# First four x tiles by row loads and TensorE turning instead of transposing loads, with new orders for all engines

## The chip, the cores and the metric

The kernel runs on one core of one Trainium2 chip. The metric is device time in microseconds (us), the median of several runs. A core has TensorE (PE, with PEld for its weight loads), VectorE (DVE), ScalarE (ACT), GpSimd (POOL) and SyncE (SP), which here only issues DMAs; ACT issues some too. Every engine works through its own list in order and waits on semaphores.

## The reference, cut to what matters

x has 2048 rows of D = 448. Part A is attention with a memory over 4 segments of 512 rows and 16 heads of 28; part B is a token-mixing MLP over normalised x; a gate mixes both.

```python
q, k, v = heads(x @ wq), heads(x @ wk), heads(x @ wv)      # 16 heads, 4 segments
p = softmax(qs @ ks.T * scale + causal_mask)               # per segment and head
a_dot = p @ vs
a_mem = (phi(qs) @ M) / (phi(qs) @ z + 1e-6)               # phi(t) = t+1 if t>0 else exp(t)
o = sigmoid(beta) * a_mem + (1 - sigmoid(beta)) * a_dot
M, z = M + phi(ks).T @ vs, z + sum(phi(ks))                # after each segment
a = o @ wo
h = layernorm(x)                                           # over D, no weights
b = (gelu(h.T @ w1 + b1) @ w2 + b2).T                      # w1: 2048 x 1792, w2: 1792 x 2048
g = sigmoid(sum(x * gate_w))
out = g * a + (1 - g) * b                                  # bf16, 1 x 2048 x 448
```

## The kernel before, in words

The kernel is one straight program. Each piece of work is an `op` with a name, the resources it reads and writes, and a body; `ORDER` lists, engine by engine, the names in the order in which they are issued. Where a name is followed by `@` and digits these are the PSUM banks or buffers it takes; `*n` repeats a name with its last number counted up. A planner outside this file, with costs and due times of its own, wrote these lists; the file only follows them and adds the semaphore waits that the resources ask for.

x is needed in two forms. Rows (`xh`, 16 tiles of 128 rows; `ldx4` loads tiles 4 to 7) feed the layer norm: `bns`, `bna` (statistics), `vpe`, `rstd`, `nmr` (coefficients) and `ln{t}`, which normalises tile t in place for the MLP. Turned (`xT`, columns of x on partitions, in four pieces c of 128 columns starting at 0, 128, 256 and 320, and four groups tc of 512 rows) it feeds the projections. Before the change `transpose_x(tc)` (L548) fills group tc by two transposing DMAs on SP, `dtx{tc}_0` (c = 0 to 2) and `dtx{tc}_1` (c = 3).

Weights: `ldwv0`, `ldwv1`, `ldwv2`, `ldwvb` (L538, L542) load wv in four parts by c on ACT's queue, `ldwk*` and `ldwq*` wk and wq, mostly on SP's; `padk`, `padx`, `padq` on DVE (L675) spread wk and wq into the padded form `wqk`. `ldgw` loads the gate's weights, `gtr` turns them on PE, `gw` copies them beside wv. `ldb1`, `ldb2` (L568, L570) load the biases on ACT's queue into a stage that `szb` on POOL clears first; `szg` clears the gate's stage; `btr` turns the biases. `v0`, `v1` set constants in the v buffer, `id0`, `id1` make the identity matrix `ident`.

PE names: `warm`, `warm2` are dummy matmuls (L664); `pra{t}`, `prb{t}`, `prt{t}` are the passes over c = 0, c = 1 and the last whole c of the value projection of row tile t; `lot{t}` is the half-row pair that does the remaining 64 rows of the contraction for tiles t and t+1 at once. `prk`, `prq`, `prx`, `lok`, `loq`, `pra0_g` are the same for keys, queries and the spread last dims. `sc` are scores (28-row tiles), `pv` probabilities times values (32-column tiles), `mst`, `mem` the memory, `u{ft}-{t}` and `y{T}-{ft}` the passes of the MLP, `lw`, `wo` the output projection. Most of them are emitted through one helper, so L296 stands for nearly all of PE's matmuls; scores are L1015, pv L1045. PE passes differ in the tile shape of the array: 128x128, 64-row halves, 28-row tiles, 32-column tiles. A stretch of 128-row passes that has a `pv` or `mst` in it is issued as 32-column tiles throughout.

After PE: `cpv`, `cpk`, `cpq` copy projections out of PSUM on ACT or DVE, `gt` is the gate's tanh (ACT), `exp` the softmax's exponentials (ACT, L1024), `mask` the causal masks (POOL), `ta`, `oa`, `om`, `ot`, `o`, `ox`, `oy` finish attention (DVE, the adds `o*` on POOL or DVE), `gsq`, `gvh`, `garg`, `gth`, `gelu` make the GELU, `ag` scales the output projection, and `fin` mixes and `out` stores (L1251, L1255).

`halves` and `both` can also run a projection pair, or single passes of the MLP and the output projection, wholly as half-row pairs: names `dt6-i`, `dk1_2-i`, `dw6-i` and `u12x-k`, `u12y-k`. They are taken when the order asks for such names; the code for them is in the kernel before as well.

Of the kernel before, what the change touches and what calls it, by code (L numbers as in the profile page):

```python
# [334 lines left out]
y5-8*2 sc6_0 y4-0@7 y5-10*4 wo6 y4-1*2 sc6_1 pv11@4 y4-3*3 y6-0@6*2 mst2@5 sc6_2 y4-6 y6-2*5 prt13@4 lot12@5 mem3
y6-7*5 y4-7*2 prt12 y4-9*2 y6-12*2 sc6_3 lot14@45 prt15 prt14 y4-11*3 sc6_4 pv12@5 y7-0@4*3 wo9@7 lw8@5 sc7_0 wo8
y7-3*7 sc7_1 y7-10*2 pv13@6 y7-12*2 y8-0@5*4 sc7_2 y8-4*2 y9-0@7*3 y8-6 wo10@6 y8-7 sc7_3 wo11@4 y8-8*4 y9-3 y8-12*2
y9-4 sc7_4 lw10 y9-5*5 pv14@5 y10-0@6*7 y9-10*2 pv15@4 y11-0@5 y10-7 y11-1*3 y10-8*2 y9-12*2 y11-4*5 y10-10*2 y11-9*3
lw12 lw14 y10-12 y11-12*2 y10-13 wo14 wo15 wo12 y12-0@4*2 wo13 y13-0@7*4 y15-0@5 y13-4*2 y14-0@6*2 y13-6*4 y12-2
# [1039 lines left out]
```

## Time and profile before

| | |
|---|---|
| time, median of 3 runs | 170.26 us (170.17 to 170.64) |
| the profiled execution | 170.1 us, its span 168.3 us |
| PE busy | 164.0 us, 97% of the span |
| DVE busy | 136.9 us, 81% |
| ACT busy | 130.4 us, 77% |
| POOL busy | 64.5 us, 38% |

The profile is of one execution; times in it count from the span's start. "Busy" of PE is from the start of a matmul to its modelled end, and matmuls overlap, so busy PE need not be PE at its peak. A row of the timeline gives start, duration, engine, line, instruction, what it writes and reads, how many instructions are merged in it, and in brackets the idle time before it with what ended it. SPq and ACTq are the issuing of DMAs, not the transfers.

### The profile page before, as it was taken

To read this page: it belongs to the slowest core of one execution; us is meant where nothing else is said; L and a number is where in the kernel's file an instruction comes from. 1 tells how busy PE (TensorE), PEld (TensorE's weight loads), DVE (VectorE), ACT (ScalarE), POOL (GpSimd) and SP (SyncE) were. 2 spreads that over 40 slices of the span, in tenths; PEclk is the share of its full clock that TensorE was granted. 3 is DMA by queue.
4 is the path that set the end of the run, shared out by engine and by line. 5 is a ranking of instruction groups with operands and counts; after the bars stand their busy time and mean duration, and the time that the engine had idled before them with its cause. 6 is when DMAs were issued, how large, how long until landed. Compare 5 with 4: busy or idle time off the path is not lost.

```text
span 168.3 us, 4931 instructions
## 1 busy us (share of the span) xinstructions
PE 164.0 (97%) x2017; PEld 77.6 (46%) x2017; DVE 136.9 (81%) x321; ACT 130.4 (77%) x164; POOL 64.5 (38%) x100
## 2 busy tenths in 40 slices
...
GB/s 144 259 225 296 242 236 237 167 220 189 181 158 221 217 101 146 163 213 126 103 108 182 67 2 63 97 77 157 253 126 84 42 63 283 225 117 27 117 27 82
DMA packets 53974, 25.44 MB, mean 151 GB/s; under 512 B 18416, under 2 KB 53712, under 8 KB 53952
## 3 DMA queue, kind: packets, MB, share of 16 engines
...
q10 hardware_dynamic: 792, 0.58, 1.6%
...
q14 instruction: 6, 0.05, 0.1%
...
## 4 chain that ended last, share of the span: by engine, by line
PE 94%; DMA 3%; ACTq 1%; POOL 0%; issue 0%; DVE 0%; POOLq 0%
PE t L296 79%; PE t L1015 8%; PE t L1045 5%; DMA t<-in_A_wv_dram 3%; PE t L896 1%; PE t L1118 1%; ACTq L538 1%; ACTq L559 0%; DVE t L1251 0%; POOL t L557 0%; POOL t L633 0%; POOL t L600 0%; PE t L927 0%; POOL t L632 0%; POOL t L628 0%
## 5 line engine op out<-in xcount | busy, mean ns | idle before, releaser
L296 PE MATMUL t<-t 128*32 128x448 bf16 (+8 forms) x1252 | 140.5, 352 | 1.1 <-DMA t<-in_A_wv_dram 1.0
L296 PEld LDWEIGHTS t<-t 128*32 128x32 bf16 (+2 forms) x1252 | 63.0, 97 | 64.3 <-issue 14.2
L1024 ACT ACTIVATE t<-t 128x2048 bf16<-128x2048 f32 x40 | 75.2, 1879 | 6.8 <-PE t L1015 6.2
L1027 POOL TENSOR_SCALAR_AFFINE_SELECT t<-t 128x512 bf16<-128x512 bf16 x64 | 43.5, 691 | 42.5 <-ACT t L1024 39.6
L1082 POOL TENSOR_TENSOR t<-t 128x448 bf16<-128x448 f32 (+2 forms) x13 | 13.3, 1026 | 19.0 <-DVE t L1075 14.4
L1251 DVE SCALAR_TENSOR_TENSOR t<-t 128x448 bf16<-128x448 f32 (+2 forms) x17 | 10.7, 645 | 10.2 <-PE t L296 10.1
L1015 PE MATMUL t<-t 28*128 28x512 bf16 (+3 forms) x256 | 15.8, 301 | 0.0
L1059 DVE STREAM_TRANSPOSE t<-t 128x512 f32<-128x512 f32 x16 | 11.3, 706 | 2.9 <-PE t L1045 2.7
L965 POOL TENSOR_TENSOR t<-t 128x4 f32<-128x4 f32 x4 | 4.2, 1054 | 23.3 <-DVE t L963 21.6
L1157 ACT ACTIVATE t<-t 128x448 bf16<-128x448 f32 x10 | 7.0, 732 | 7.7 <-PE t L296 7.7
L1045 PE MATMUL t<-t 128*32 128x512 bf16 (+3 forms) x256 | 11.5, 299 | 0.0
L1101 DVE STREAM_TRANSPOSE t<-t 128x512 bf16<-128x512 bf16 x16 | 10.9, 690 | 0.0
L1015 PEld LDWEIGHTS t<-t 28*128 28x128 bf16 x256 | 4.4, 92 | 14.0 <-ACT t L1024 7.7
L956 DVE BATCH_NORM_STATS2 t<-t 128x6 f32<-128x448 bf16 x16 | 9.3, 610 | 1.1 <-DMA t<-in_A_x_dram 1.1
L857 ACT ACTIVATE t<-t 128x448 bf16<-128x448 f32 x13 | 6.8, 546 | 4.2 <-PE t L296 4.2
L1220 DVE SCALAR_TENSOR_TENSOR t<-t 128x448 f32<-128x448 f32 x14 | 9.2, 664 | 0.5 <-ACT t L1215 0.4
L1045 PEld LDWEIGHTS t<-t 128*32 128x32 bf16 x256 | 6.7, 97 | 5.3 <-issue 0.4
L1212 ACT ACTIVATE t<-t 128x448 f32<-128x448 f32 x14 | 8.8, 638 | 0.1
L818 ACT ACTIVATE t<-t 128x512 bf16<-128x512 bf16 x12 | 7.6, 635 | 1.4 <-DVE t L775 1.4
L847 DVE SCALAR_TENSOR_TENSOR t<-t 128x512 bf16<-128x512 bf16 x12 | 8.5, 712 | 0.1
L1075 DVE SCALAR_TENSOR_TENSOR t<-t 128x448 f32<-128x448 f32 x12 | 8.4, 698 | 0.0
L1225 DVE SCALAR_TENSOR_TENSOR t<-t 128x448 bf16<-128x448 f32 x14 | 8.4, 614 | 0.0
...
## 6 DMA issues: line engine op xcount, KB each, us to landing
...
```

Source lines behind the costliest of these rows:

```text
L296: last = e.matmul(out[q], w[:, q], x, skip_group_check=True, **kw)
L956: op("DVE", lambda e: e.bn_stats(st6[:, t, :], xh[:, t, :]), reads=[R_x[t]], writes=[R_st6[t]], name=f"bns{t}", cost=512, prio=P_PROJ - 10 ...
L1015: last = e.matmul(bank(hl)[:, c0 : c0 + w], kT[r, hg, s * 512 + j * 128 : s * 512 + j * 128 + 128], qT[r, hg, s * 512 + 128 * j : s * 512 ...
L1024: exps.append(op("ACT", lambda e: e.activation(pslot(g), ps[:, 0:4, :], ACT.Exp, scale=SCALE), reads=R_bank[0:4], writes=[g.res], take=g, ...
L1027: op("POOL", lambda e, c0=c0: e.affine_select(pslot(g)[:, :, c0 : c0 + 128], pslot(g)[:, :, c0 : c0 + 128], pattern=[[0, 4], [1, 128]], co ...
L1045: last = e.matmul(bank(cb)[32 * ((hl + hg) % 4) : 32 * ((hl + hg) % 4) + 32, 128 * j : 512], vaug[:, 4 * s + j, 32 * h : 32 * h + 32], psl ...
L1059: dv(lambda e: e.transpose(tt[:, ia, :], bank(cb)[:, 0:512]), [bres(cb)], [R_tt[ia]], "ta", 630, use=(cb,))
L1082: return e.tensor_tensor(dst, part(n3[0]), part(n3[1]), op=ALU.add)
L1101: dv(lambda e: e.transpose(oT[:, hg, s * 512 : s * 512 + 512], o), [R_ob[hg]] + ([R_obx] if hg else []), qres(hg, s), "ot", 635)
L1212: op("ACT", lambda e: e.activation(gg[:, q, :], bank(b)[:, 0:D], ACT.Square, bias=b1s[:, ft : ft + 1], scale=math.sqrt(GC)), **buse(b), re ...
L1220: op("DVE", lambda e: e.scalar_tensor_tensor(gg[:, q, :], gg[:, q, :], 1.0, vh[:, q, :], op0=ALU.add, op1=ALU.mult), reads=[R_gg[q], R_vh[ ...
L1251: op("DVE", lambda e: e.scalar_tensor_tensor(outst[:, p, c0:c1], bank(b)[:, 0 : c1 - c0], omg[:, T : T + 1], ag(T)[:, c0:c1], op0=ALU.mult ...
```

## The change

The two transposing DMAs of group 0 go. `ldx0` and `ldx2` load row tiles 0, 1 and 2, 3 as the first two DMAs of SP's queue. PE turns them by matmuls against the identity in four steps `xt{p}_{k}` (p: row tiles 2p and 2p+1; k: pieces c = 2k and 2k+1), each four matmuls of 128 columns into one PSUM bank. A copy `cx{p}_{k}` brings each bank into `xT` (three on ACT, `cx0_1` on DVE in the new order). The resource of `xT` group 0 now has four parts instead of two, and the first passes wait for their part only (`xres`, `rx`). `ldx0` used to be one load of tiles 0 to 3 later in SP's queue. `ldwv2`, `ldwvb` and `ldwkb` move from ACT's queue to SP's. There are eight dummy matmuls ahead of the turning instead of nine and a tenth after `gtr`. All five orders are new: among other things `szb` goes from first to seventh on POOL, `btr` later, four `bns` come at the start of DVE's list, the value passes of row tiles 4 to 9, one pair of key passes, and some passes of the MLP and the output projection use the half-row forms, nine `o*` adds move from POOL to DVE, and drains and `ag` are dealt out anew between ACT and DVE.

```diff
@@ -317,75 +317,89 @@
 ORDER = {
     "PE": """
-warm gtr@4 warm2 pra0@5 pra1@6 pra2@7 pra3@4 prb3 prb2 prb0 prb1 lot2 lot0 prt1 prt3 prt2 prt0 pra0_1 pra0_2 pra0_0
-btr@5 lok0_0 lok0_2 prk0_0 prx0_3 prk0_2 prk0_1 prt7@7 prx1_3@4 prk1_2@6 lot6@5 lok1_2 loq0_0 loq0_2 prq0_2 prq0_0
...
+warm xt0_0 gtr@4 xt0_1 xt1_0 xt1_1 pra1@5 pra0@6 prb0 prb1 pra2@7 prb2 pra3@4 prb3 lot2 lot0 prt2 pra0_2 prt0 prt1
+prt3 pra0_0 pra0_1 lok0_2 lok0_0 prk0_1 prx0_3 prk0_0 dt6-4@65 dk1_2-4@47*2 dt6-5 dk1_2-6 loq0_0 dt6-6 dk1_2-1*2
+dt6-1*3 dk1_2-0 dk1_2-3 dt6-0 prq0_1 prk0_2 prq1_0@4 prq0_0 loq0_2 loq1_0@5 btr@6 prq1_1 prq0_2 prq1_2h@7 prq0_2h
...
+prk2_0@5 lok2_2@7 lok2_0 sc0_2 prx2_3 u1-3@4 u1-0 u0-10@5 u0-8 u1-6 u1-5 u1-10 u1-2 u0-6 sc0_3 u1-12 u1-4 u0-3 u0-12
...
     "ACT": """
-ldwv0 ldgw ldwv1 ldwv2 ldwvb ldwkb ldb1 ldb2 cpv2 cpv0 gt0 gt2 cpv1 gt3 gt1 ek0_0 cpk0_1 cpk0_3 cpq0_3 ek0_1 cpv7 gt7
...
+ldwv0 ldgw ldwv1 ldb1 ldb2 cx0_0 cx1_0 cx1_1 gt0 gt1 gt3 cpv2 gt2 cpk0_0 ek0_0 cpq0_3 cpk1_2 cpv7 gt7 gt6 cpk1_3
...
     "DVE": """
-ob0 gw padk0 padx0 cpv3 padk1 padx1 padk2 padx2 padq0 padq1 b2c padq2 b1c padq3 cpk0_0 cpk0_2 mk0_0 bns3 bns1 bns0
...
+ob0 bns0 gw bns3 bna0 cx0_1 bns2 padk0 padx0 bna2 bns1 padk2 bna3 bna1 padk1 padx2 cpv0 padq1 padq0 padx1 cpv3 cpv1
+cpk0_1 vpe0 padq3 padq2 cpk0_3 gcol0 nmr0 ln3 ln1 mk0_0 bns4 bns7 cpv6 cpk0_2 ln0 bna4 bns6 bns10 bns5 bns8 bna7 b2c
...
     "POOL": """
-szb szg mhalf oo0 og0 id0 oo1 v0 v1 og1 id1 rstd0 rstd4 og2 mask0_0_0 rstd8 mask0_1_1 mask0_1_3 rstd12 oo2 mask0_4_1
...
+mhalf szg v0 v1 id0 id1 szb rstd0 oo0 rstd8 rstd4 rstd12 oo1 og0 oo2 og1 mask0_2_2 og2 mask0_0_0 mask0_1_1 mask0_3_0
...
     "SP": """
-dtx0_0 dtx0_1 ldwk0@0 ldwk1 ldwq0@1 ldwqb dtx1_0 dtx1_1 ldx0 ldx4 ldx8 ldbeta ldw1_0_0 dtx2_0 ldx12 dtx2_1 ldw1_0_1
...
+ldx0 ldx2 ldwv2 ldwvb ldwk0@0 ldwk1 ldwkb ldwq0@1 ldwqb dtx1_0 dtx1_1 ldx4 ldx8 ldbeta ldw1_0_0 dtx2_0 ldx12 dtx2_1
...
@@ -497,7 +511,12 @@
     slots = [wown[:, i, :] for i in range(NSL)]
 
     R_x = R("x", NT)
-    R_xT = [R(f"xT{t}_", 2) for t in range(4)]
+    R_xT = [R(f"xT{t}_", 4 if t == 0 else 2) for t in range(4)]
+
+    def xres(tc, cs=range(NCT), halves=range(2)):
+        return [R_xT[0][k] for k in sorted({2 * p + c // 2 for p in halves for c in cs})] if tc == 0 else \
+            [R_xT[tc][k] for k in sorted({c // 3 for c in cs})]
+
     R_phk = [R(f"phk{s}_", NHG) for s in range(3)]
     R_kphi = R("kphi", 2)
     R_wkp, R_wqp = R("wkp", 6), R("wqp", 4)
@@ -535,7 +554,7 @@
 
     def load_w(dst, src, r, name, take=None, last="SP"):
         for k, (c0, c1) in enumerate({4: ((0, 1), (1, 2), (2, 3)), 3: ((0, 2), (2, 3)), 2: ((0, 3),)}[len(r)]):
-            op("ACT" if len(r) == 4 else "SP", lambda e, c0=c0, c1=c1: e.dma_start(
+            op("ACT" if len(r) == 4 and k < 2 else "SP", lambda e, c0=c0, c1=c1: e.dma_start(
                 dst()[:, c0:c1, 0:D], src[128 * c0 : 128 * c1].rearrange("(c p) d -> p c d", p=128)),
                writes=[r[k]], name=f"ld{name}{k}", dma=True, prio=-3, cost=500, nbytes=114688 * (c1 - c0),
                take=None if k else take)
@@ -549,9 +568,10 @@
                 xT[:, c : c + n, tc * 512 : tc * 512 + 512], x2[tc * 512 : tc * 512 + 512, C0[c] : C0[c] + 128 * n]),
                writes=[R_xT[tc][k]], name=f"dtx{tc}_{k}", dma=True, cost=1200 * n, nbytes=227000 * n, prio=(-3, -3, -1, 0)[tc])
 
-    transpose_x(0)
-    load_w(lambda: wvx, WV, R_wv, "wv", None, "ACT")
-    load_w(wk_nat, WK, R_wk, "wk", P_wk, "ACT")
+    load_x("SP", 0, 2)
+    load_x("SP", 2, 2)
+    load_w(lambda: wvx, WV, R_wv, "wv", None, "SP")
+    load_w(wk_nat, WK, R_wk, "wk", P_wk, "SP")
     load_w(wq_nat, WQ, R_wq, "wq", P_wq, "SP")
     for st, rs, name in ((gstage, R_gst, "g"), (bstage, R_bst, "b")):
         op("POOL", lambda e, st=st: e.memset(st[:].bitcast(U32), 0), writes=rs, name="sz" + name, cost=100, prio=-5.0)
@@ -559,7 +579,6 @@
     op("ACT", lambda e: e.dma_start(gstage[0:6, :], gview), writes=R_gst, name="ldgw", dma=True, prio=-3, cost=500,
        nbytes=2000)
     transpose_x(1)
-    load_x("SP", 0, 4)
     load_x("SP", 4, 4)
     load_x("SP", 8, 4)
     load_x("SP", 12, 4)
@@ -667,8 +686,32 @@
 
         op("PE", fn, writes=[R_bank[3]], name=name, mode="f", cost=n * pe_cost(512), prio=prio, rel=rel)
 
-    warm_up(9, "warm", -1)
-    warm_up(1, "warm2", P_PROJ + 0.01, 3500.0)
+    def turn_x():
+        for p in range(2):
+            for k in range(2):
+                b = 2 * p + k
+
+                def fn(e, p=p, k=k, b=b):
+                    for c in (2 * k, 2 * k + 1):
+                        for t in range(2):
+                            at = 256 * (c % 2) + 128 * t
+                            last = e.matmul(bank(b)[:, at : at + 128], xh[:, 2 * p + t, C0[c] : C0[c] + 128], ident[:, :],
+                                            start=True, stop=True, skip_group_check=True)
+                    return last
+
+                op("PE", fn, reads=R_x[2 * p : 2 * p + 2] + [R_ident], writes=[R_bank[b]], name=f"xt{p}_{k}", mode="f",
+                   cost=pe_cost(128, 128, 128, 128), prio=-1)
+
+                def ends(p=p, k=k, b=b):
+                    return (xT[:, 2 * k : 2 * k + 2, 256 * p : 256 * p + 256],
+                            bank(b).rearrange("p (c t) -> p c t", c=2))
+
+                op("ACT", lambda e, ends=ends: e.activation(*ends(), ACT.Copy), reads=[R_bank[b]], writes=[R_xT[0][b]],
+                   name=f"cx{p}_{k}", cost=act_cost(512), prio=-1,
+                   alt=("DVE", lambda e, ends=ends: e.tensor_copy(*ends()), dve_cost(512)))
+
+    warm_up(8, "warm", -1)
+    turn_x()
 
 
     def pad_w(name, src, c0, c1, s0, s1, d0, d1, f0, use, reads, write):
@@ -760,10 +803,10 @@
 
     def proj_d(name, R_w, G, tc, t0, n, out):
         ts = slice(tc * 512 + t0, tc * 512 + t0 + n)
-        need = R_xT[tc]
+        need = xres(tc)
         return dict(n=n, w=lambda c, rows: wqk[rows, c, 4 * G : 4 * G + 4, :].rearrange("p h j -> p (h j)"),
                     x=lambda c, rows: xT[rows, c, ts], need=need + R_w, use=xuse(tc).get("use", ()),
-                    by=lambda c: [need[c // 3]] + [R_w[k] for k in range(len(R_w)) if R_w[k] not in R_wkp or k % 3 == (0, 0, 1, 2)[c]],
+                    by=lambda c: xres(tc, (c,)) + [R_w[k] for k in range(len(R_w)) if R_w[k] not in R_wkp or k % 3 == (0, 0, 1, 2)[c]],
                     name=name + ("h" if t0 else ""), out=out)
 
     def do_k(tc, hg, t0=0, n=512):
@@ -776,7 +819,7 @@
 
         P = proj_d(f"prk{tc}_{hg}", R_wkp, hg, tc, t0, n, out)
         if tc == 0:
-            P["first"] = [((0, 1), [R_xT[0][0], R_wkp[0], R_wkp[3]])]
+            P["first"] = [((0, 1), xres(0, (0, 1)) + [R_wkp[0], R_wkp[3]])]
         return P
 
     def do_x(tc):
@@ -860,13 +903,15 @@
             op("ACT", lambda e: e.activation(gth[:, t : t + 1], bank(b)[:, D : D + 1], ACT.Tanh, scale=0.5),
                **buse(b), reads=[bres(b)], writes=[R_gth[t]], name=f"gt{t}", cost=60, prio=P_BASE)
 
-        rx = R_xT[t // 4]
+        def rx(cs=range(NCT)):
+            return xres(t // 4, cs, (t % 4 // 2,))
+
         P = dict(n=D + 1, w=lambda c, rows: xT[rows, c, t * 128 : t * 128 + 128],
-                 x=lambda c, rows: wvx[rows, c, 0 : D + 1], need=rx + R_wv + [R_gw],
-                 by=lambda c: [rx[c // 3], R_wv[c], R_gw],
+                 x=lambda c, rows: wvx[rows, c, 0 : D + 1], need=rx() + R_wv + [R_gw],
+                 by=lambda c: rx((c,)) + [R_wv[c], R_gw],
                  use=xuse(t // 4).get("use", ()), name=f"prt{t}", out=out)
         if t < 4:
-            P["first"] = [((0,), [rx[0], R_wv[0], R_gw]), ((1,), [R_wv[1]])]
+            P["first"] = [((0,), rx((0,)) + [R_wv[0], R_gw]), ((1,), rx((1,)) + [R_wv[1]])]
         return P
 
     def do_gw():
```

More of the change, by code (lines that the diff above doesn't have):

```diff
@@ L335 @@
[L335 to L339, printed above, removed]
@@ L367 @@
-gcol3 b2g2 eps12 omg3 rec12 oa12 fin6 ag8 om12 ta13 ot12 rec13 fin7 om13 oa13 o13 ot13 eps14 fin8 ag10 ta14 rec14 om14
-oa14 ta15 rec15 om15 oa15 b2g3 fin9 ot14 ot15 fin11 fin10 fin13 fin12 fin14 fin15 fin15#1""",
-    "POOL": """
-szb szg mhalf oo0 og0 id0 oo1 v0 v1 og1 id1 rstd0 rstd4 og2 mask0_0_0 rstd8 mask0_1_1 mask0_1_3 rstd12 oo2 mask0_4_1
-mask0_4_3 mask0_3_0 mask0_2_2 mask1_1_1 mask0_2_2#1 mask1_1_3 mask1_2_2 mask1_2_2#1 mask1_0_0 oy0 ox0 mask2_0_0
-mask1_3_0 mask1_4_1 mask1_4_3 mask2_2_2 mask2_2_2#1 mask2_1_1 mask2_1_3 mask2_3_0 mask2_4_1 mask2_4_3 mask3_0_0
@@ new lines @@
+y7-11 y9-5 y7-0 y7-4 y8-12@4 y8-7 y9-10 y9-4 y6-10 y8-0 y9-9 sc6_4 y7-10 y7-2*2 y8-13 y8-4 y8-2 wo9@6 lw8@5 sc7_0
+y8-10 wo8 y8-1 y8-8 pv12@6 y9-6 pv13@5 y9-13 y8-11 y9-2 sc7_1 y9-12 y8-9 y8-6 y10-2@6 y9-1 y10-11 y10-7 y10-9 y11-11@5
+y8-3 y10-4 y11-12 y8-5 sc7_2 y11-9 y11-0 wo10@7 y11-2 wo11@4 y10-3 y10-0 sc7_3 y10x-6 y10x-8 y10x-10 y10x-5 y10x-13
+lw10 y10y-13 y10y-10 y10y-5*2 y10y-8 sc7_4 y11-4 pv14@7 y12-4@4 y10-1 y11-3 y10-12 y12-1 y11-7 y13-0@7 y13-4 y13-12
+y12-11 y13-7 y11-1 y13-3 y15-9@6 y13-8 y15-5 y15-4 y12-8 pv15@5 y13-6 y13-1 y12-3 y12-6 y15-12 y12-7 y14-2@5 y15-2
@@ new lines @@
+y12-0 y13-10 lw14 lw12 y14-8 y15-8 y15-13 y13-2 y12-10 y15-0 y15-11 y14-11 y15-10 y12-13 y12-9 y15-7 y15-1 y13-5
+y13-11 y12-12 y15-6 y12-2 y14-4 y12-5 y13-13 y14-9 y13-9 wo13 y14-0 wo15 wo12 y14-12 y15-3 y14-1 y14-3 wo14 y14-13
+y14-10 y14-5 y14-7 y14-6 y15-1#1@7 y15-9#1 y15-10#1 y15-4#1 y15-6#1 y15-7#1 y15-2#1 y15-12#1 y15-11#1 y15-3#1 y15-5#1
+y15-0#1 y15-13#1 y15-8#1""",
+    "ACT": """
+ldwv0 ldgw ldwv1 ldb1 ldb2 cx0_0 cx1_0 cx1_1 gt0 gt1 gt3 cpv2 gt2 cpk0_0 ek0_0 cpq0_3 cpk1_2 cpv7 gt7 gt6 cpk1_3
```

112 lines of the change are left out of this document (62 added, 50 removed).

## The prediction

> **What bounds the kernel now.** I read the page first, then the busy time by stretches, then the first 16 us in order of time, because the change touches the loads at the start and otherwise only re-orders work.
>
> ```profile
> span 168.3 us, 4931 instructions
> PE 164.0 (97%) x2017; PEld 77.6 (46%) x2017; DVE 136.9 (81%) x321; ACT 130.4 (77%) x164; POOL 64.5 (38%) x100
> PE 94%; DMA 3%; ACTq 1%; POOL 0%; issue 0%; DVE 0%; POOLq 0%
> ```
>
> The first row gives the span, the second the busy time by engine, the third the chain that ended last: 94% of it is TensorE and 3% a load. The stretches say where TensorE is not full (columns: window, its length, busy us and instruction count of PE, PEld, DVE, ACT, POOL, then clock, DMA share, GB/s):
>
> ```profile
> 0.00:7.43 7.43, 5.50 (x21) 2.02 (x21) 0.45 (x2) 1.28 (x1) 2.20 (x15) 1.00 0.85 182
> 7.43:20.00 12.57, 12.57 (x74) 5.48 (x75) 9.95 (x32) 9.61 (x25) 0.54 (x1) 1.00 1.06 258
> ...
> 60.00:120.00 60.00, 60.00 (x818) 28.32 (x811) 56.83 (x123) 56.88 (x68) 27.65 (x37) 1.00 0.51 119
> 120.00:166.00 46.00, 45.94 (x594) 23.12 (x592) 32.92 (x64) 23.60 (x23) 17.29 (x24) 1.00 0.40 119
> 166.00:168.30 2.30, 0.00 (x0) 0.00 (x0) 0.33 (x1) 0.00 (x0) 0.00 (x0) 1.00 0.19 50
> ```
>
> From 7.43 us to the last matmul TensorE is never seen idle, so a new order can win there only by fewer passes, fewer changes of tile shape, or pauses too short to show (ends are modelled). What is left to win is before 7.43 us. That stretch, and what follows it:
>
> ```profile
> 0.78 0.38 ACTq L538 DMA_DIRECT2D t<-in_A_wv_dram  x1
> 0.78 0.24 POOL L557 MEMSET t<- 128x64 uint32 x2 [0.29 <-POOLq L1364]
> 0.79 2.67 SPq L548 DMA_TRANSPOSE t<-in_A_x_dram  x2
> 0.82 3.38 PE L664 MATMUL t<-const-bfloat16-1.0 128*128 128x512 bf16 x9 [0.82 <-PEq L1364]
> 1.20 0.73 ACTq L559 DMA_DIRECT2D t<-in_gate_w_dram  x1
> 1.46 1.11 POOL L626 MEMSET t<- 128x256 uint32 x2
> 1.96 0.94 ACTq L538 DMA_DIRECT2D t<-in_A_wv_dram  x2
> 2.60 0.29 POOL L601 TENSOR_SCALAR_AFFINE_SELECT t<-t 128x128 bf16<-128x128 bf16 x1
> 3.51 1.08 SPq L538 DMA_DIRECT2D t<-in_A_wk_dram  x2
> 4.24 0.45 ACTq L568 DMA_DIRECT2D t<-in_B_b_dram  x1
> 4.59 0.92 PE L296 MATMUL t<-t 128*128 128x449 bf16 x4
> 4.71 0.37 ACTq L570 DMA_DIRECT2D t<-in_B_b_dram  x1
> 5.12 1.28 ACT L857 ACT_TABLE_LOAD   x1 [5.12 <-issue]
> 5.91 0.93 PE L296 MATMUL t<-t 128*128 128x449 bf16 x4 [0.40 <-DMA t<-in_A_wv_dram]
> 7.43 2.78 PE L296 MATMUL t<-t 64*128 64x449 bf16 x14 [0.59 <-DMA t<-in_A_wv_dram]
> 8.59 0.62 DVE L859 CAST t<-t 128x448 bf16<-128x448 f32 x1
> 8.70 0.98 ACT L857 ACTIVATE t<-t 128x448 bf16<-128x448 f32 x2 [2.30 <-PE t L296]
> 10.07 1.68 SPq L533 DMA_DIRECT2D t<-in_A_x_dram  x3
> 10.86 0.98 PEld L296 LDWEIGHTS t<-t 128*128 128x128 bf16 x6 [0.23 <-issue]
> ```
>
> Useful matmuls begin at 4.59 (pra, four passes), stop for wv's second part until 5.91 (prb, four passes), and stop again until 7.43 (the half-row pair lot2). Four passes take 0.92, of which the last's own 0.35 is its depth, so a pass of 449 columns takes 0.19; I use 0.216 for 512 columns (0.19 x 512/449). Eight passes are 1.52, so of the 2.84 us from 4.59 to 7.43 1.3 is waiting for transfers:
>
> ```profile
> PEld t L296 <- DMA t<-in_A_x_dram: 1.4, 2, 1.0
> PE t L296 <- DMA t<-in_A_wv_dram: 1.0, 2, 0.6
> DMA to landing us min/median/max: 2.1/4.4/5.1
> ```
>
> The last row is for the wv, wk and wq loads of L538: 2.1 us from issue to landing at best (the first, with the queue empty), 4.4 at the median.
>
> **The change, part by part.** *Loads.* The two transposing loads (2.67 us of SP's queue) go. In front of dtx1_0 SP now issues ldx0, ldx2, ldwv2, ldwvb and ldwkb besides wk and wq. A row load takes 0.56 to issue (1.68 for three), the weight parts 0.54 (1.08 for two): 2 x 0.56 + 3 x 0.54 = 2.74, so dtx1_0 is issued when it was; from ldx4 on each is one issue, 0.56, earlier, and ACT's queue loses three issues. x0 (224 KB) should land at 0.79 + 2.1 plus what 112 KB more takes beside wv0, by 3.0 to 3.8; x2 some 0.9 later; wv2 and wvb, issued near 2.0 and 2.5, near 5. None of these is last, as follows.
>
> *Dummies.* Eight instead of nine and one. The eighth ends the wait of PE's queue near 3.8 us, when x0 has landed. Priced at nothing: PE would wait anyway.
>
> *Turning.* 16 matmuls of 128 columns and four copies out of PSUM. The price of a 128-column pass:
>
> ```profile
> L296 PE MATMUL t<-t 128*128 128x128 bf16 x14 | 0.9, 219 | 0.0
> ...
> 12.56 0.58 ACT L773 ACTIVATE t<-t 128x512 bf16<-128x512 f32 x1
> 101.98 1.88 ACT L1024 ACTIVATE t<-t 128x2048 bf16<-128x2048 f32 x1 [0.55 <-PE t L1015]
> 103.91 0.12 PEld L1015 LDWEIGHTS t<-t 28*128 28x128 bf16 x8 [0.42 <-ACT t L1024]
> ```
>
> (0.9 - 0.22)/13 = 0.05 each, 0.9 us in all; the first two steps are done by 4.3, the last two by about 5.0 after x2. They fill PE's wait. A copy of 512 columns takes ACT 0.58, and PE starts 0.05 after an ACT instruction ends (101.98 + 1.88 = 103.86, weights at 103.91).
>
> So ACT decides. Its queue is ldwv0, ldgw, ldwv1 (to 1.96 + about 0.37 = 2.33), then ldb1 and ldb2, then the table load, then cx0_0. ldb1 has a wait that is new in effect: it needs szb, which POOL did first and now does last of seven: 0.78 + two or three small memsets 0.35 + v0, v1 1.11 + id0 0.2 + id1 0.29 puts szb at about 2.75. Queued behind ldb1 are ldb2, the table load and all copies. So ldb1 2.8, ldb2 to 3.65 (0.45 + 0.37), table 3.7 to 4.97 (1.28), cx0_0 5.0 to 5.6, pra1 at 5.68, which is 1.1 later than before's first pass. But then it no longer stops: pra1, pra0, prb0, prb1 need only cx0_0, the next four only cx1_0, which ends by 6.2, and cx1_1 and DVE's cx0_1 end before the pair. 5.68 + 1.52 + 0.10 for the change to half rows = 7.30 against 7.43: **-0.13**. Bounds: if POOL is no hindrance and ldb1 goes at 2.33, everything is 0.5 earlier (-0.6); if issues on ACT take 0.6 each, 0.3 later (+0.2).
>
> *From the pair to the first pass after lok0_2 and lok0_0.* Before this took 7.43 to 10.86, 3.43. The passes are 2 + 4 of 449 and 6 + 2 of 512 columns, 1.14 + 1.73, and three changes of shape 0.3: 3.18. The rest was waiting for wq and for the small btr, which moves later. New order: lok0_2 needs padx1, which on DVE stands behind cpv0, and cpv0 waits for prt0; cpv0 8.8 to 9.4 (0.62), three pads of 0.15, so 9.9, and PE comes at 9.96. It just fits: **-0.2** (0 to -0.25).
>
> *Half-row forms.* The `d...` and `x/y` steps replace whole passes by pairs of half-row passes; both orders need the same pass times (seven per pair either way). A change of shape costs:
>
> ```profile
> 20.73 0.39 PE L1015 MATMUL t<-t 28*128 28x512 bf16 x4
> 21.06 2.48 PE L296 MATMUL t<-t 64*128 64x512 bf16 x13
> ```
>
> four score matmuls run at once and the next shape starts 0.33 later instead of 0.216: 0.11. Counted through the orders from lot2 on, with the rule that a stretch holding a pv or mst runs as 32-column tiles, there are 111 changes before and 110 after: **-0.1**. So the many new half-row steps win nothing by themselves; if a pair costs 0.01 more than a pass, the 58 more cost up to +0.6 (the score rows give 0.33 for four at once, so I take 0).
>
> *Moved work.* DVE's list grows from 321 to 340 (nine adds from POOL, cx0_1, drains and ag from ACT, some back), POOL's falls by nine, ACT's activations by six in spite of three copies.
>
> ```profile
> L956 DVE BATCH_NORM_STATS2 t<-t 128x6 f32<-128x448 bf16 x16 | 9.3, 610 | 1.1 <-DMA t<-in_A_x_dram 1.1
> L1082 DVE TENSOR_TENSOR t<-t 128x448 bf16<-128x448 f32 x1 | 0.6, 625 | 0.0
> 27.39 0.40 DVE L972 TENSOR_SCALAR t<-t 128x448 bf16<-128x448 bf16 x1
> ```
>
> 19 x 0.62 = 12 us more on an engine with 168.3 - 136.9 = 31 idle: 88% busy. Four of the sixteen statistics (0.61 each) come before 7 us, when DVE had nothing. The tight place is the normalised x: before, ln5 ended at 27.79 and its matmul u1-5 came about 0.5 later. In the new lists DVE's instructions to ln5 add up (group means, 0.06 off each for overlap) to 23.3 us from 3.5, so 26.8 without idling; PE reaches u1-5 20.8 after the pair, at 28.1 less the 0.2 won. DVE idles at least 0.6 for prt0. That leaves 0 to 0.5. I take **+0.2** for new waits here and later (0 to +1.2: a tenth of the 12 us, if DVE comes last).
>
> *End.* fin15#1 and its store follow the last matmul as before; y14 now ends just ahead of it and fin14 (0.65) fits into the 14 passes (0.78). 0, up to +0.2 for the two stores together.
>
> **Sum.** -0.13 - 0.2 - 0.1 + 0.2 = -0.23. The profiled execution took 170.1 (span 168.3 and 1.8 around it), the runs' median is 170.26, 0.16 more. 170.26 - 0.23 = 170.0; I put **169.9**, since the bounds of the start reach further down. That is within 0.3% (0.5 us), about what a measurement of this kernel can tell from no change.
>
> **Rivals.** *Faster: the table is no gate.* If cx0_0 starts as soon as xt0_0 is through (4.2), pra1 comes at 4.85 and the pair at 6.5: -0.95, with -0.3 from the next two terms 169.0; half of it, with ldb1 at 2.33, gives 169.4. For it: the table load at 5.12 did not wait for the matmuls that its first instruction needed. Against it: it did stand behind ldb2 in the queue (4.71 + 0.37 = 5.08).
>
> *Slower: DVE becomes last.* It decides once its lead at ln5 is gone, that is when it idles over 1 us before 28 us or its instructions take 5% longer than the means. Each later instruction then passes its delay to PE; a tenth of the 12 us on the path gives 171.2. For it: DVE 56.83 of 60 in the middle. Against: ACT, which was as full, is relieved, and four statistics come early.
>
> *Slower: a pause after the table load.* The first activation before came at 8.70, 2.30 after the load's end, and is put down to PE; a pause of ACT's own of anything from 0 to 2.3 would not have shown. From it the first copy decides as soon as it is over zero. Half of it, 1.15, puts the pair at 8.45 and the time at 171.1. For it: nothing excludes it. Against it: the row shows no second instruction between load and activation. [...]
>
> *No gain at the start.* With ACT's issues at 0.6 each the pair is at 7.6, 0.2 late, and only the wait for wq is won: 170.2 to 170.4. This lies in my case's own range.
>
> **How the numbers follow.** My case (169.6 to 170.6 by itself) 0.43; the faster rival in whole or by half 0.34; DVE last 0.16; the pause after the table 0.07. Faster by over 0.3% 0.34, within 0.43, slower 0.23. Range: down to 169.0 (rival without the gate), up to 171.2 (either slow rival), with about 1 in 10 left on each side.
>
> **What would show it.** Right: no transposing load before 5.6 us; the table load near 3.7 and the first copy right behind it near 5.0; the first 449-column pass near 5.7; PE's pair near 7.3; after it PE full. Wrong: a first copy before 4.6 or after 5.6; waits of PE for DVE near 28 us or in the middle; DVE's share away from 88%; a clock below 1.00 after fewer dummies, which would cost 1.5 on the first eight passes.

## Result, and the profile after

The changed kernel takes 171.63 us in the median (171.18 to 173.25, 12 runs) against 170.40 (170.17 to 170.94) for the kernel before on the same chip: ratio 1.0080, interval 1.0060 to 1.0099. It is slower by 0.8%, 1.2 us. The prediction was 169.9 with a range of 169.0 to 171.2: the sign was wrong, and the time lies above the range. Four executions of all those below took 209 to 326 us, three of them at a granted clock of 0.66 to 0.76; medians and ratios leave them out, and the kernel with `go1_0` undone, whose profiled execution is one of them, has no row in the table of profiles below.

The profiled execution is the slowest of the runs, 173.25 us with a span of 171.4. Span, busy times and the chain that ended last, from its page:

```profile
span 171.4 us, 4958 instructions
PE 166.0 (97%) x2023; PEld 78.9 (46%) x2023; DVE 149.5 (87%) x340; ACT 127.9 (75%) x158; POOL 58.7 (34%) x91
PE 74%; DVE 16%; DMA 5%; POOL 1%; ACT 1%; SPq 1%; issue 0%
```

The share of PE in the chain fell from 94% to 74%. The shares of the others are not the cost: the chain is followed back from each wait through whatever ran before it, so a wait of 0.5 us can put several us of DVE into the list. What the waits themselves cost stands in the list of PE's waits (engine and line, what it waited for, total us, times, longest):

```profile
PE t L296 <- DMA t<-t: 0.8, 1, 0.8
PE t L296 <- DMA t<-in_B_w_dram: 0.5, 1, 0.5
PE t L1090 <- POOL t L1072: 0.4, 1, 0.4
PE t L296 <- DVE t L1017: 0.3, 1, 0.3
```

Four single waits for four different things. The stretches place them (same columns as before the change). The first row is 20 to 60 us of the kernel before, which the prediction left out; the others are the changed kernel in the same windows:

```profile
20.00:60.00 40.00, 40.00 (x522) 18.70 (x521) 36.41 (x104) 39.02 (x50) 16.81 (x25) 1.00 0.87 203
...
0.00:7.43 7.43, 6.59 (x32) 3.57 (x33) 3.41 (x11) 2.96 (x4) 1.89 (x11) 1.00 0.77 232
7.43:20.00 12.57, 12.57 (x85) 5.53 (x84) 10.95 (x37) 7.19 (x19) 1.40 (x2) 1.00 1.10 236
20.00:60.00 40.00, 39.12 (x480) 17.94 (x479) 37.57 (x100) 36.80 (x47) 16.95 (x26) 1.00 0.79 187
60.00:120.00 60.00, 59.16 (x808) 27.84 (x809) 56.98 (x117) 55.37 (x67) 23.24 (x32) 1.00 0.44 117
120.00:166.00 46.00, 45.56 (x603) 22.14 (x598) 37.72 (x75) 24.18 (x21) 15.19 (x21) 1.00 0.39 115
```

Before, PE was full from 7.43 on; now 0.9, 0.8 and 0.4 us are missing in the last three. The four places, from the timeline of the changed kernel:

```profile
31.03 0.59 DVE L1025 TENSOR_SCALAR t<-t 128x4 f32<-128x4 f32 x1
31.54 0.68 DVE L818 CAST t<-t 128x512 bf16<-128x512 f32 x1
32.14 0.38 DVE L1017 TENSOR_SCALAR t<-t 128x448 bf16<-128x448 bf16 x1
32.58 0.55 PE L296 MATMUL t<-t 128*128 128x448 bf16 x2 [0.33 <-DVE t L1017]
...
50.15 1.17 SPq L567 DMA_TRANSPOSE t<-in_A_x_dram  x1
52.38 0.38 SPq L607 DMA_DIRECT2D t<-in_B_w_dram  x1
52.81 0.54 SPq L842 DMA_DIRECT2D spare_heads<-t  x1
53.39 1.00 SPq L607 DMA_DIRECT2D t<-in_B_w_dram  x2
58.32 0.56 PE L296 MATMUL t<-t 128*32 128x448 bf16 x8 [0.51 <-DMA t<-in_B_w_dram]
...
105.90 0.67 SPq L1150 DMA_DIRECT2D t<-t  x1
107.99 0.92 SPq L607 DMA_DIRECT2D t<-in_B_w_dram  x2
111.43 1.23 SPq L868 DMA_TRANSPOSE t<-t  x1
112.70 0.52 SPq L842 DMA_DIRECT2D spare_heads<-t  x1
113.27 0.64 SPq L1150 DMA_DIRECT2D t<-t  x1
117.08 0.36 PE L296 MATMUL t<-t 64*128 64x448 bf16 x2 [0.84 <-DMA t<-t]
...
122.28 2.03 POOL L1072 TENSOR_SCALAR_AFFINE_SELECT t<-t 128x512 bf16<-128x512 bf16 x2 [0.41 <-ACT t L1069]
124.37 0.73 PE L1090 MATMUL t<-t 128*32 128x512 bf16 x16 [0.44 <-POOL t L1072]
```

`u1-7` waits for `ln7` (L1017, 32.14), which stands on DVE behind `omg0` (L1025) and `cpk2_1` (L818). `u9-5` waits for one part of w1's fifth block, `ldw1_4_1` (part 1 of 0 to 3; the expectations below call it the fourth). SP issues it first in the row of 53.39, behind a store (`gk2_3`, L842) and behind `ldw1_5_1`, ahead of which SP issued nothing from 51.32 to 52.38. `lw4` waits for `go1_0`, the second half of a transfer of `oT` into the half-row form: its twin `go1_1` is issued at 105.90, it itself only at 113.27. Five other issues stand between (the expectations say four), and SP issues nothing from 108.91 to 111.43, ahead of a transposing one. `pv11` waits for its mask, the second of the row of 122.28.

The bracket counts from the modelled end of the pass before. Counted from start to start, less the pass itself (0.19 for 448 columns, 0.216 for 512) and 0.1 for a change of shape (from the pass at 10.26 to the half-row pair at 10.57 it is 0.31, 0.216 of it the pass), PE lost 0.49, 0.70, 0.90 and 0.62: 2.7 us in this execution, the slowest of the twelve.

The start, from the timeline of the changed kernel (before's stands in the prediction):

```profile
3.42 1.28 ACT L709 ACT_TABLE_LOAD   x1 [3.42 <-POOL t L577]
4.21 0.63 PE L698 MATMUL t<-t 128*128 128x128 bf16 x4
4.73 1.44 PE L698 MATMUL t<-t 128*128 128x128 bf16 x12
4.88 0.60 ACT L709 ACTIVATE t<-t 128x512 bf16<-128x512 f32 x1 [0.17 <-PE t L925]
5.96 2.80 PE L296 MATMUL t<-t 128*128 128x449 bf16 x13
7.91 0.12 PEld L296 LDWEIGHTS t<-t 64*128 64x128 bf16 x4 [0.37 <-issue]
```

The sixteen turning passes take 0.107 each, not 0.05 (twelve of them 1.44, less the depth of the last), and the pair lot2 starts at 7.92 instead of 7.43. Pitch is the time from the start of one pass to the start of the next. Single starts of the matmuls show that the 512-column dummies were 0.43 apart ("half pitch" below: half as fast), and that passes came at their full pitch (0.22 for 512 columns) only from 6.6 us on; in the profile of before the dummies went from 0.43 to 0.22 apart at 3.5 us. The granted clock reads 1.00 in both; where the expectations below speak of a clock that rises, this change of pitch is what the traces show.

### The profile page after: what moved, and what is told of

The parts are those of the page before. It is cut to its first block, busy times and chain, and to the rows that moved or that the text cites. A ratio compares the mean times of both kernels' runs of the same rounds, so it can differ in the third digit from the quotient of the medians.

```text
span 171.4 us, 4958 instructions
## 1 busy us (share of the span) xinstructions
PE 166.0 (97%) x2023; PEld 78.9 (46%) x2023; DVE 149.5 (87%) x340; ACT 127.9 (75%) x158; POOL 58.7 (34%) x91
## 4 chain that ended last, share of the span: by engine, by line
PE 74%; DVE 16%; DMA 5%; POOL 1%; ACT 1%; SPq 1%; issue 0%
PE t L296 60%; PE t L1060 6%; PE t L1090 4%; DVE t L1001 3%; DMA t<-in_B_w_dram 3%; DVE t L1017 3%; DMA t<-t 2%; PE t L683 2%; DVE t L1171 1%; POOL t L1072 1%; DVE t L818 1%; ACT t L1069 1%; DVE t L1146 1%; DVE t L865 1%; PE t L698 1%; PE t L1163 1%
## 5 line engine op out<-in xcount | busy, mean ns | idle before, releaser
L296 PE MATMUL t<-t 128*32 128x448 bf16 (+11 forms) x1244 | 141.2, 352 | 1.7 <-DMA t<-t 0.8
L1072 POOL TENSOR_SCALAR_AFFINE_SELECT t<-t 128x512 bf16<-128x512 bf16 x64 | 45.5, 729 | 70.5 <-ACT t L1069 70.0
L1202 ACT ACTIVATE t<-t 128x448 bf16<-128x448 f32 x6 | 4.2, 722 | 11.6 <-PE t L296 11.6
L1104 DVE STREAM_TRANSPOSE t<-t 128x512 f32<-128x512 f32 x16 | 11.4, 711 | 1.3 <-PE t L1090 1.1
L1146 DVE STREAM_TRANSPOSE t<-t 128x512 bf16<-128x512 bf16 x16 | 10.8, 687 | 1.3 <-POOL t L1127 1.3
L1010 POOL TENSOR_TENSOR t<-t 128x4 f32<-128x4 f32 x4 | 4.7, 1184 | 20.5 <-DVE t L1008 20.0
L1206 DVE TENSOR_SCALAR t<-t 128x448 bf16<-128x448 f32 x10 | 7.3, 741 | 3.7 <-PE t L296 3.7
L1265 DVE SCALAR_TENSOR_TENSOR t<-t 128x448 f32<-128x448 f32 x14 | 8.7, 632 | 0.9 <-ACT t L1260 0.8
L1127 POOL TENSOR_TENSOR t<-t 128x448 bf16<-128x448 f32 x4 | 4.9, 1236 | 11.9 <-DVE t L1122 11.9
L1171 DVE STREAM_TRANSPOSE t<-t 128x512 f32<-128x512 f32 x12 | 7.7, 689 | 1.4 <-PE t L1163 1.3
L1120 DVE SCALAR_TENSOR_TENSOR t<-t 128x448 f32<-128x448 f32 x12 | 8.4, 704 | 0.0
```

The costliest lines, as they stand in the source:

```text
L296: last = e.matmul(out[q], w[:, q], x, skip_group_check=True, **kw)
L1072: op("POOL", lambda e, c0=c0: e.affine_select(pslot(g)[:, :, c0 : c0 + 128], pslot(g)[:, :, c0 : c0 + 128], pattern=[[0, 4], [1, 128]], co ...
L1104: dv(lambda e: e.transpose(tt[:, ia, :], bank(cb)[:, 0:512]), [bres(cb)], [R_tt[ia]], "ta", 630, use=(cb,))
L1146: dv(lambda e: e.transpose(oT[:, hg, s * 512 : s * 512 + 512], o), [R_ob[hg]] + ([R_obx] if hg else []), qres(hg, s), "ot", 635)
L1171: op("DVE", lambda e, b=b, t=t: e.transpose(t, bank(b)[:, 0:512]), reads=[bres(b)], writes=[R_tt[2 + hg]], name=f"tm{u}", cost=630, prio=pr)
```

## The experiments

Theory O: the loss is the four waits, that is, places in the new orders. Rival S: it is the start at half pitch. Rival D, from the prediction: DVE, with 19 instructions more, has become the bound.

**Copies of both kernels.** The kernel before again, and the changed one again.

> The kernel before, unchanged, for a second profile. If the clock's rise is fixed to the first matmul, the pitch of the 512-column dummies halves at about 3.5 us again; if it depends on the run, it falls elsewhere between 2 and 7 us. Either way the pair lot2 should start at 7.4 +- 0.15, because the passes ahead of it wait for wv; no interior wait over 0.2 us. Span 168.0 to 168.8.

> The changed kernel, unchanged. Theory O (the waits stand in the new orders): the waits at u1-7 (0.49 for DVE), u9-5 (0.70 for a load of w1), lw4 (0.90 for a load behind SP's queue) and pv11 (0.62 for POOL's mask) come back in the second profile within 0.3 each; median 171.0 to 171.8. Theory S (the start decides: the clock rises late in the profiled run): pair at 7.4 to 7.5 where the clock is full by 4 us, 7.9 where it comes at 6.6; interior waits are the same in both and the time scatters by 0.5 with the rise. If the interior waits were chance of the slowest run, they are mostly gone here and the span is under 170.

Before: full pitch from 4.1 us, pair at 7.01, span 168.6. One wait of 0.87 for a padded weight behind the pair ate the earlier start; so neither the pair at 7.4 nor "no interior wait over 0.2" came true. The changed kernel: median 171.76 (171.09 to 172.26), ratio 1.0087 (1.0067 to 1.0108). Its profiled run took 171.09, and the start had turned round:

```profile
4.21 0.48 PE L698 MATMUL t<-t 128*128 128x128 bf16 x4
4.58 0.83 PE L698 MATMUL t<-t 128*128 128x128 bf16 x12
4.73 1.58 ACT L709 ACTIVATE t<-t 128x512 bf16<-128x512 f32 x3
5.38 3.29 PE L296 MATMUL t<-t 128*128 128x449 bf16 x17
7.01 0.11 PEld L296 LDWEIGHTS t<-t 64*128 64x128 bf16 x4 [0.37 <-issue]
```

With the full pitch from 4.4 us the same instructions put the pair at 7.01, 0.9 earlier than in the first profile. Yet this run too was 0.7 over before: the waits at lw4 (0.60) and pv11 (0.63) were back, u1-7 had 0.17 and u9-5 0.07. Together that is 1.5 us, against 2.7 in the first profile and 1.2 to 1.4 between the medians of the two kernels. So the expectation "within 0.3" held for two sites and failed for the two early ones, and in this run the start could not be the loss.

**The start alone.** Row loads, turning passes and eight dummies; every other order as before:

```diff
 "PE":  -warm gtr@4 warm2 pra0@5 pra1@6 pra2@7 pra3@4 prb3 prb2 prb0 prb1 lot2
        +warm xt0_0 gtr@4 xt0_1 xt1_0 xt1_1 pra0@5 pra1@6 prb0 prb1 pra2@7 prb2 pra3@4 prb3 lot2
 "SP":  -dtx0_0 dtx0_1 ldwk0@0 ldwk1 ldwq0@1 ldwqb dtx1_0 dtx1_1 ldx0 ldx4
        +ldx0 ldx2 ldwv2 ldwvb ldwk0@0 ldwk1 ldwkb ldwq0@1 ldwqb dtx1_0 dtx1_1 ldx4
 "ACT": -ldwv1 ldwv2 ldwvb ldwkb ldb1 ldb2 cpv2
        +ldwv1 ldb1 ldb2 cx0_0 cx1_0 cx1_1 cpv2
 "DVE": -gw padk0
        +gw cx0_1 padk0
```

> The new start alone: row loads of x0 and x2, identity passes, eight dummies; all engines' orders otherwise as in the kernel before (POOL's too, so its memset for the ldb1 wait comes first). Theory O: 169.6 to 170.6, within 0.3 % of before, and no interior wait over 0.3 us beyond those of before. Theory S: slower by 0.4 to 0.9 (170.8 to 171.3), with the pair at 7.9 or later and full pitch only after 6 us. Rival D (DVE's load, +19 instructions): no slower than before, as DVE gets only one copy here.

170.34 (169.80 to 170.60), ratio 0.9996 (0.9981 to 1.0011): no change, although its profile had the full pitch only from 6.7 us and the pair at 8.01. From the pair to the last pass it took 158.10, before 158.30. Rival S is refuted: the new start by itself costs the median nothing, and even the profiled run, whose start was later than any of the changed kernel's, took only 170.56.

**Four mends.** The changed kernel with four places of its orders mended; in the last, `mst2` moves ahead of `y4-8` as well:

```diff
 SP:  -ldws1 dtx3_1 ldw1_5_1 gk2_3 ldw1_4_1        +ldw1_4_1 ldws1 dtx3_1 ldw1_5_1 gk2_3
 SP:  -go1_1 gk3_3 ldw2_3_2 ldw2_3_0 tk2_2 gq3_3 go1_0    +go1_1 go1_0 gk3_3 ldw2_3_2 ldw2_3_0 tk2_2 gq3_3
 DVE: -ln9 omg0 cpk2_1 ln7                         +ln9 ln7 omg0 cpk2_1
 PE:  -pv10@5 y4-8 pv11@6 mst2@7 y4-11             +pv10@5 mst2@7 y4-8 y4-11 pv11@6
```

> The changed kernel with four places of its orders mended: the load go1_0 two places earlier on SP (for lw4), the fourth part of w1's fifth block ahead of its neighbours on SP (for u9-5), ln7 ahead of omg0 and cpk2_1 on DVE (for u1-7), pv11 after three other passes (for the mask). Theory O: the four waits shrink from 2.7 us to under 0.8 and the time falls by 1.0 to 2.5, to 169.0 to 170.6. Theory S: it falls by under 0.5, to 171.0 or more, as the start is the same. Rival D: only the ln7 mend counts, the time falls by 0.2 to 0.5 and DVE waits come up at other passes.

170.16 (169.72 to 170.59), ratio 0.9994 (0.9982 to 1.0005): 1.6 us under the changed kernel beside it, all of the loss. Its page and its list of PE's waits:

```profile
PE 164.4 (98%) x2018; PEld 78.9 (47%) x2023; DVE 149.3 (89%) x340; ACT 127.8 (76%) x158; POOL 59.4 (35%) x91
PE 98%; issue 0%; DVE 0%
...
PE t L683 <- PEq L1409: 0.8, 1, 0.8
PE t L296 <- issue: 0.5, 3, 0.2
PE t L296 <- ACT t L816: 0.2, 1, 0.2
```

The four waits are gone and none took their place; the chain is PE to 98%. The gaps put down to "issue" and to ACT stand where this profile lacks the record of a 512-column pass (2018 records against 2023 in the changed kernel's first profile, which shows no such gap), so they are not read as waits. DVE is as loaded as in the changed kernel (149.3 against 149.5 us, 340 instructions): rival D is refuted. What SP does for lw4 now, and PE there:

```profile
104.35 1.34 SPq L1150 DMA_DIRECT2D t<-t  x2
...
112.80 2.17 PE L296 MATMUL t<-t 128*128 128x448 bf16 x11
114.90 0.39 PE L1060 MATMUL t<-t 28*128 28x512 bf16 x4
```

Both halves are issued in one go, and passes and scores follow each other without the gap of 117.08.

**One mend at a time.**

> The changed kernel with one mend: the load go1_0 directly behind go1_1 on SP instead of behind four more issues. If lw4's wait (0.90 and 0.60 us in the two profiles of the changed kernel) is the place of go1_0 in SP's queue, that wait goes and the time falls by 0.5 to 0.9 us, to 170.9 to 171.3; if the transfer itself is late (its source or its memory traffic), the wait stays and the time with it.

> The changed kernel with one mend: pv11 two passes and the mst2 stretch later. Its wait for the mask was 0.62 and 0.63 in the two profiles. If the waits add, the time falls by 0.4 to 0.65, to 171.1 to 171.4; if pv11 only shows a delay that another place would take over, by under 0.2.

> The changed kernel with the two early mends: ln7 ahead of omg0 and cpk2_1 on DVE, the fourth part of w1's fifth block earlier on SP. These waits were 0.49 and 0.70 in one profile, 0.17 and 0.07 in the other. If they add to the late ones, the time falls by 0.2 to 1.2. If lw4's wait behind them is set by SP's clock time, what is won early is lost there again: time falls by under 0.2, and lw4's wait grows by what is won. If DVE's load was the loss (rival), this mend alone brings it back, by 1.0 or more.

Ratios to before: 1.0089 (1.0069 to 1.0109), 1.0065 (1.0052 to 1.0078) and 1.0062 (1.0037 to 1.0086), against 1.0087 without a mend. The store mend won nothing in the median though its wait was gone in the trace; the other two won about 0.4 us each. Together that is 0.8 of 1.6. PE's longest waits in the profiles of the mask mend, then of the two early mends:

```profile
PE t L296 <- DMA t<-in_B_w_dram: 1.0, 1, 1.0
PE t L296 <- DMA t<-t: 0.7, 1, 0.7
...
PE t L296 <- DVE t L1146: 0.5, 1, 0.5
PE t L1090 <- POOL t L1072: 0.4, 1, 0.4
```

The wait for w1 is not the same from run to run: 1.17 from start to start in the first of these two kernels, 0.07 and 0.70 in the two profiles of the changed one. With so much scatter from that site a single mend of another is hard to see in five or six runs. In the second, lw4's wait is put down to the transpose ahead of its transfer (L1146); it was 0.52, not the 0.60 plus what was won early that the second theory wanted.

**One mend undone at a time**, on the steadier base of the four:

> The four mends less one: go1_0 is back at its later place on SP. With the other three waits gone, lw4 should wait 0.6 to 0.9 us and the time be 170.16 + 0.6 to 0.9 = 170.8 to 171.1. If the wait at lw4 is only taken over from elsewhere (the single mend of it won nothing in the median), the time stays within 0.2 of four mends.

> The four mends less one: pv11 is back right behind pv10 and y4-8. It waited 0.62 to 0.63 in each profile where it stood there: time 170.16 + 0.6 = 170.8; if passes behind it waited anyway, under 170.4.

> The four mends less one: the fourth part of w1's fifth block stands behind its three neighbours on SP again. u9-5's wait was 0.07, 0.66, 0.70 and 1.17 in the four profiles that had this order: 0.65 in the mean, time 170.2 to 171.3 with a median near 170.8, and a wider scatter of the runs than four mends' 0.9. If the scatter of the changed kernel came from the clock at the start, the scatter stays 0.9.

> The four mends less one: ln7 stands behind omg0 and cpk2_1 on DVE again. u1-7's wait was 0.49, 0.17, 0 and 0 in the four profiles with this order, most where the pair came last: 0.15 in the mean, time 170.1 to 170.5. If DVE's load were the loss (rival), this one alone brings back 1.0 or more.

| undone | median us | ratio to before (95%) | against four mends (0.9994) |
|---|---|---|---|
| go1_0 on SP (lw4) | 170.90 | 1.0028 (1.0012 to 1.0045) | +0.34%, 0.6 us |
| pv11 (mask) | 170.37 | 1.0006 (0.9990 to 1.0022) | +0.12%, 0.2 us |
| w1's part on SP (u9-5) | 170.52 | 1.0017 (0.9997 to 1.0037) | +0.23%, 0.4 us |
| ln7 on DVE (u1-7) | 170.10 | 0.9987 (0.9971 to 1.0003) | -0.07%, 0.1 us less |

By the medians SP's two places make up 1.0 of the 1.6 us, the mask 0.2, DVE nothing that shows; only go1_0's interval lies clear of that of four mends (0.9982 to 1.0005), so the other shares are estimates. The mask mend was expected at 0.6 and its wait did come back in the trace (0.62); only a third of that is in the median. In its profile the wait does count from the pair on (158.73 against 158.19 us in the table below), but the pair there came 0.45 earlier than in four mends'. Singles and undos sum to 0.8 and 1.1 us, all four to 1.6; with intervals of 0.2 us and more on each side, I cannot say whether the rest is noise or waits that hide each other. Undoing w1's place widened the runs to 169.75 to 171.29, as expected. But the early mends, which have that place mended, scatter just as widely (170.71 to 172.05 in six runs), so what makes the changed kernel scatter stays open.

**What the profiles add up to.** The first half-row matmul and the last matmul bound a stretch with no start in it (counted from start to start; "rest" is that stretch less the waits):

| kernel | pair at | pair to last pass | waits at u1-7, u9-5, lw4, pv11 | rest |
|---|---|---|---|---|
| before, four profiles | 7.43, 7.01, 7.25, 7.54 | 158.30, 159.01, 158.24, 158.16 | none (0.87 elsewhere in the second) | 158.1 to 158.3 |
| changed, first | 7.92 | 160.83 | 0.49, 0.70, 0.90, 0.62 | 158.1 |
| changed, second | 7.01 | 159.59 | 0.17, 0.07, 0.60, 0.63 | 158.1 |
| store mend | 7.36 | 159.45 | 0, 0.66, 0, 0.63 | 158.2 |
| mask mend | 7.16 | 160.10 | 0, 1.17, 0.73, 0 | 158.2 |
| early mends | 7.01 | 159.28 | 0, 0, 0.52, 0.63 | 158.1 |
| mask undone | 7.08 | 158.73 | 0, 0, 0, 0.62 | 158.1 |
| w1 undone | 7.22 | 158.80 | 0, 0.64, 0, 0 | 158.2 |
| ln7 undone | 7.16 | 158.36 | 0.18, 0, 0, 0 | 158.2 |
| four mends | 7.53 | 158.19 | none | 158.2 |

Without the four waits every kernel takes the same 158.1 to 158.3 us from the pair on. In these profiles that is the whole difference of the orders.

**The start by itself.** Four mends with the zeros for ldb1 second on POOL and seven dummies; four mends with twelve dummies; the kernel before twice more; and the first of these with ln7 left where the change put it.

```diff
 POOL: -mhalf szg v0 v1 id0 id1 szb rstd0     +mhalf szg szb v0 v1 id0 id1 rstd0
       -warm_up(8, "warm", -1)                +warm_up(7, "warm", -1)      (the other kernel: 12)
```

> The four mends and a shorter start: POOL sets the zeros that ldb1 waits for as its second memset instead of its seventh, and seven dummies instead of eight. Table load at 3.1 to 3.2 instead of 3.43, xt0_0 when x0 has landed (4.0 to 4.25). If ACT's table sets the start, the pair comes 0.25 earlier than with four mends at the same rise of the clock, and the time is 169.7 to 170.1. If TensorE's slow clock in the sixteen turning passes sets it, the pair moves with the clock's rise alone: 7.0 where that is at 4.4, 7.5 to 8.0 where it is at 5.9 or later; time within 0.2 of four mends.

> Four mends with twelve dummies instead of eight, so four more passes of 512 columns ahead of the first turning pass. If the rise of the clock is a matter of chance with about the scatter seen (3.5 to 6.7 us), the dummies end at 5.0 (rise at 4.0) to 6.0 (rise after 6), the pair lies at 7.4 to 8.5, 0.3 to 0.9 later than with eight, and the time is 170.3 to 171.1. If the turning passes held the clock down, it rises by 4.2 here and the pair is at 7.4 to 7.6, the time 170.1 to 170.4. If dummies cost nothing, as predicted, 170.0 to 170.3.

> The kernel before, a third profile. Chance: the rise may fall anywhere from 3.5 to 6.7 us. A property of the new start: it falls at 3.5 to 4.2 again. The pair at 7.0 to 7.6 either way, if the passes ahead of it wait for wv; later than 7.6 if a late clock reaches it here too.

> The kernel before, a fourth profile, with the same expectation as the third: rise anywhere from 3.5 to 6.7 us by chance, 3.5 to 4.2 if the late rise belongs to the new start; pair at 7.0 to 7.6.

> The shorter start (zeros for ldb1 second on POOL, seven dummies) with three mends, ln7 left where the change put it, since undoing that mend cost nothing (0.9987 against 0.9994 of before). Expected 169.9 to 170.1, a ratio of 0.998 to 0.999. If the new start's term of -0.13 us holds once the waits are gone, the ratio's interval lies below 1; if the start is worth nothing on average, it is 0.999 to 1.0005 and holds 1.

Shorter start: 170.05, ratio 0.9990 (0.9976 to 1.0003), pair at 7.27 with the full pitch from 5.6 us. With three mends: 170.10, 0.9987 (0.9971 to 1.0003), pair at 7.34. These, four mends and ln7 undone all lie at 0.9987 to 0.9994 of before, none with an interval that excludes 1: if there is a gain, it is some 0.2 us. Twelve dummies: 170.59, 1.0016 (0.9998 to 1.0034), pair at 8.84; so dummies are not free: four more hold the first turning pass back from 4.20 to 5.91 and cost 0.4 us in the median, though the interval still touches that of four mends. PE in that kernel, then in the third profile of before:

```profile
0.84 5.28 PE L683 MATMUL t<-const-bfloat16-1.0 128*128 128x512 bf16 x12 [0.84 <-PEq L1409]
5.91 0.60 PE L698 MATMUL t<-t 128*128 128x128 bf16 x4
7.20 1.13 PE L296 MATMUL t<-t 128*128 128x449 bf16 x5
...
0.82 4.00 PE L664 MATMUL t<-const-bfloat16-1.0 128*128 128x512 bf16 x9 [0.82 <-PEq L1364]
5.22 3.08 PE L296 MATMUL t<-t 128*128 128x449 bf16 x14
```

Twelve dummies all ran at 0.43 and the full pitch came at about 6.3 us. The kernel before had it from 5.9 us in its third profile (its nine dummies take 4.00 instead of 3.38) and from 3.7 in the fourth: the late rise is no property of the new start. But before the change it cost nothing that shows: the pair came at 7.25 with the late rise, at 7.43 and 7.54 with the early ones. In the early ones PE waits for wv's transfer (1.0 and 0.8 us in the first and fourth profile); in the third the slower passes fill that time, and no such wait is in its list.

## Why the prediction was wrong, by its steps

**Moved work, +0.2 (0 to +1.2): the step that failed.** It should have been +1.6, which is what the four mends bring back. I priced the new orders by DVE's load alone and bounded them by a tenth of DVE's added 12 us. DVE's load was foretold well (88%; 87 to 88% measured), and cost next to nothing: its one wait (u1-7) is 0.5 us at most, and undoing its mend shows no loss. The loss sits where no step of mine looked: SP's list past 10 us, where a load and a transfer stand behind other issues (1.0 us of the 1.6 by the medians, 0.6 of it clear of noise), and a mask on an engine that is 34% busy. The tight place I named, u1-5 near 28 us, did not wait. That from 7.43 us on "a new order can win there only by fewer passes" was read for the gain and not turned round: where no pass waits, a new order can only bring waits in.

**Rival "DVE becomes last", 171.2.** The time was nearly right and the mechanism wrong: four mends run with DVE at 89% and chain PE 98%. I gave this side 0.16 for one engine and nothing for the queues.

**Start, -0.13, pair at 7.30.** In the mean of the twelve profiles with the new start and seven or eight dummies the pair is at 7.34, from 7.01 to 8.01; in those of before at 7.31. The table load came at 3.42 (I said 3.7), the first copy at 4.88 (5.0): the queue of ACT was read rightly, and the wait for POOL before it is in the row. What failed is that ACT always decides and that turning and dummies are free: at half pitch PE decides, 16 turning passes take 1.75 us from 4.21 to 5.96 instead of 0.9. That the mean pair lies so near to 7.30 is luck: the table came 0.28 early, and the half pitch took it back. I took the pass's price from the trace's late rows and the clock from the granted value, though the quoted row of nine 512-column dummies in 3.38 us shows that they did not run at the 0.216 each, 1.9 in all, of the later rows. A granted clock below 1.00 after fewer dummies, named among the signs against me, did not come: it read 1.00 in all seventeen profiles, those with seven, eight and twelve among them; the 1.5 us beside it was an estimate of mine, the eight passes (1.52) at half their rate.

**Rivals on the table.** "No gate" did not come true: in the second profile of the changed kernel, with the pitch full at 4.4, the first copy still follows the table load by 0.03 us. The pair is at 7.01 there, 0.29 before the forecast, because the table load came 0.28 before it. "A pause after the load" is refuted: load 3.42 + 1.28 = 4.70, first copy at 4.73 in the second profile of the changed kernel.

**Pair to first pass after lok0_2 and lok0_0, 3.18.** Measured 7.92 to 11.10, 3.18, with 3.30 to 3.43 in the three profiles of before without the wait of 0.87: right to the hundredth. **Shape changes, -0.1.** No sign of it: from the pair on, the mended orders take as long as the old ones (table), so the 0.1 to 0.25 won at lok0 went again somewhere behind it; no run shows where. No cost of the half-row pairs shows either, as taken (158.19 us from the pair to the last pass in four mends, 158.16 to 158.30 in the three profiles of before without that wait). **Loads:** SP's issues took 0.43 to 0.48 and not 0.54 to 0.56, so `dtx1_0` came at 5.26 and not at 5.6; nothing followed from that. **End, 0:** nothing seen.

Without the moved work my sum is -0.43; the mended kernels say -0.1 to -0.2.
